# One level of Strassen's algorithm for the first products of seven batches, with other products between its steps

## Chip, cores, metric

One core of a Trainium2 chip. The metric is the device time of one execution in microseconds. "Faster" or "slower" means by over 2%.

## The reference

Cross attention between tokens and a small state, then a two-layer network on all rows, in f32.

```python
B, H, S, Ns, D = 8, 8, 512, 32, 64                 # x: (8,8,512,64), state: (8,8,32,64)
a = softmax(x @ state.T / sqrt(D)); xread = a @ state
a2 = softmax(state @ x.T / sqrt(D)); sread = a2 @ x
rows = concatenate([xread, sread], axis=2)         # then (B,H,S,D) -> (B*S, 512)
h = rows @ w_in                                    # 512 -> 2048
g = h * erf(softplus(h))
out = g @ w_out                                    # 2048 -> 512
```

The kernel never forms xread. For each batch it multiplies state and w_in once (a "mixed" product, `m`), so that the **first product** of a batch is h = a x m with a contraction of 256, and the **second product** is g x w_out. Both are large; Softplus, Erf and the multiplication lie between them.

## The kernel before

TensorE (PE) works through units: one unit is (batch, half of the tokens, half of the hidden features), four a batch. In a unit the first product is made tile by tile (`hidden`), then Softplus, Erf and the multiplication follow on ACT and DVE, and meanwhile PE does the second product of the unit before (`project7`, already by Strassen: 7 products for 8). Instructions are written in order of importance; the building step moves some of them ahead where it expects an engine to wait, and fixes one order for each engine.

```python
def mixed_part(b, g, j, parts):                    # L253, L255: two PSUM banks of the pool "at" (2)
    ps = [ps_at.tile([P, gw], F32, name="at")[:, 0:n] for _ in range(2)]
    for i in range(NI):
        for e in range(2):
            ...
            nc.tensor.matmul(out=ps[e][q, :], lhsT=stT[b][r, q], rhs=w_in[r, fs, i, :], ...)
    return nc.scalar.copy(mg[:, 0], ps[0]), nc.vector.tensor_copy(mg[:, 1], ps[1])

def hidden(b, fts, t0, n, copies=(nc.vector.tensor_copy,) * 4):
    ...
    for i in range(4):
        hp = ps_h.tile([P, S], F32, name="h")      # pool of 2 banks
        for j in range(m):
            ...                                    # two matmuls of 256 columns
        banks.append((nc.scalar.activation(out=s[:, i, :], in_=hp, func=ACTF.Softplus),
                      copies[i](hs[:, i, :], hp), on_pe))
    def finish():
        return (nc.scalar.activation(out=s, in_=s, func=ACTF.Erf),
                nc.vector.tensor_tensor(s, s, hs, op=ALU.mult))

def project7(gT, hs, g, first, last, acc):
    A11, A12, A22, S1, S2, S3, S4 = combine_g(gT, hs)     # four DVE sums of 128x512
    for lhs, rhs, bank, c in ((A11, B11, 2, 0), (A12, B21, 0, 0), (A22, T[4], 1, 0),
                              (S2, T[2], 0, 1), (S3, T[3], 2, 1), (S1, T[1], 1, 1),
                              (S4, B22, 3, 0)):
        for i in range(GF):
            nc.tensor.matmul(...)                  # 256 columns

# the loop over units
gT_ = first()
gT_[2]()                                           # Erf, multiplication
pending()                                          # second product of the unit before (and, every
...                                                # other time, store7: 5 DVE additions, 1 ACT copy)
if b + 1 < B:
    mixed(b + 1, g)                                # one mixed product after each unit
    if g == 1:
        attention(b + 1)[0]()
```

## Time and profile before

809.8 us is the median of four runs (808.86 to 810.66). A group is: line, engine, operation, output<-inputs, shape, count | busy us, mean ns of one | idle time ahead of it and what ended it.

```profile
L270 PE MATMUL h<-aT,m 128*128 128x256 f32 (+1 forms) x960 | 241.7, 399 | 4.5 <-DVE hs L273 2.5
...
L253 PE MATMUL at<-w_in,stT 64*32 64x512 f32 (+1 forms) x528 | 37.2, 588 | 0.7 <-ACT m L255 0.5
```

The first products are 30% of the span. The mixed products take 37.2 us of PE.

### The profile page before, as it was taken

Reading aid. Unit: us, or ns where it says so; the run is one execution under the profiler, and the core shown is the slowest. Engines: PE = TensorE matmul, PEld = TensorE weight load, DVE = VectorE, ACT = ScalarE, POOL = GpSimd, SP = SyncE. Lnnn points to the kernel's source line nnn. Section 1 sums busy time; section 2 is a strip of 40 time slices with the busy share of each in tenths; the row PEclk is TensorE's granted clock in tenths of the full one; section 3 lists DMA queues with packets and bytes.
Section 4 is the critical chain, followed back from the end, with each engine's and each line's share of the span. In section 5 each row is a group of like instructions: output and inputs, shape, how many; then the busy total and the mean of one; then the engine's idle time right before and its main releaser. Section 6 shows DMA issues by size and latency. Waiting matters only on the chain.

```text
span 810.8 us, 10642 instructions
## 1 busy us (share of the span) xinstructions
PE 792.5 (98%) x4532; PEld 611.7 (75%) x4532; DVE 427.9 (53%) x624; ACT 369.3 (46%) x466; POOL 0.7 (0%) x6
## 2 busy tenths in 40 slices
PE   8988999999999999999999999999999999999997
PEld 6533445687888788878887888878887888888886
DVE  3888854546454744555453844455455745443431
ACT  5858544655343733354334533373334533333220
POOL 0000000000000000000000000000000000000000
PEclk9999999999999999999999999999999999999999
DMA  6665521203000020003000200000000000000000
GB/s 211 208 229 186 126 49 56 53 1 79 0 27 1 8 71 1 27 1 78 1 27 1 47 32 1 27 1 27 1 27 0 27 1 26 1 27 1 26 1 26
DMA packets 47414, 35.27 MB, mean 44 GB/s; under 512 B 36872, under 2 KB 36872, under 8 KB 47368
## 3 DMA queue, kind: packets, MB, share of 16 engines
q1 hardware_dynamic: 45256, 34.09, 13.6%
q10 hardware_dynamic: 2112, 0.52, 0.3%
q8 instruction: 35, 0.57, 0.3%
q14 instruction: 11, 0.09, 0.0%
HBM read 25.69 MB, written 8.91 MB: 43 GB/s over the span
## 4 chain that ended last, share of the span: by engine, by line
PE 88%; ACT 3%; DVE 1%; DMA 1%; issue 1%; SPq 0%
PE o L335 45%; PE h L270 29%; PE o L283 5%; PE at L253 4%; PE at L156 1%; DMA raw<-in_moe_w_in_dram 1%; PE at L214 1%; PE at L226 1%; PE at L179 1%; PE at L197 1%; ACT L272 1%; ACT s L276 0%; ACT s L272 0%; ACT L276 0%; ACT xT L158 0%
## 5 line engine op out<-in xcount | busy, mean ns | idle before, releaser
L270 PE MATMUL h<-aT,m 128*128 128x256 f32 (+1 forms) x960 | 241.7, 399 | 4.5 <-DVE hs L273 2.5
L270 PEld LDWEIGHTS h<-aT,m 128*128 128x128 f32 x960 | 178.0, 190 | 67.5 <-issue 32.8
L273 DVE COPY hs<-h 128x512 f32<-128x512 f32 x134 | 91.9, 690 | 185.2 <-ACT s L272 185.1
L272 ACT ACTIVATE s<-h 128x512 f32<-128x512 f32 x136 | 80.2, 597 | 160.5 <-PE h L270 159.9
L277 DVE TENSOR_TENSOR s<-s,hs 128x2048 f32<-128x2048 f32 x34 | 77.9, 2293 | 75.8 <-ACT s L276 75.7
L335 PE MATMUL o<-w_out,s 128*128 128x256 f32 x480 | 114.9, 380 | 1.6 <-DVE s L277 1.6
L335 PE MATMUL o<-raw,hs 128*128 128x256 f32 x480 | 115.6, 380 | 0.0
L335 PE MATMUL o<-w_out,hs 128*128 128x256 f32 x480 | 113.4, 379 | 0.0
L335 PEld LDWEIGHTS o<-w_out,s 128*128 128x128 f32 x480 | 90.2, 190 | 14.3 <-DVE s L277 2.5
L335 PEld LDWEIGHTS o<-w_out,hs 128*128 128x128 f32 x480 | 91.1, 190 | 12.3
L335 PEld LDWEIGHTS o<-raw,hs 128*128 128x128 f32 x480 | 90.3, 190 | 12.4
L255 ACT COPY m<-at 128x512 f32<-128x512 f32 (+1 forms) x33 | 18.9, 573 | 154.1 <-PE at L253 154.0
L276 ACT ACTIVATE s<-s 128x2048 f32<-128x2048 f32 x34 | 64.9, 1910 | 0.4
L283 PE MATMUL o<-w_out,s 128*128 128x512 f32 x128 | 59.2, 600 | 0.9 <-DVE s L277 0.9
L335 PE MATMUL o<-raw,s 128*128 128x256 f32 x240 | 56.7, 379 | 0.0
L272 ACT ACT_TABLE_LOAD x40 | 51.3, 1283 | 0.7
L335 PEld LDWEIGHTS o<-raw,s 128*128 128x128 f32 x240 | 45.2, 190 | 5.9
L255 DVE COPY m<-at 128x512 f32<-128x512 f32 (+1 forms) x33 | 22.3, 675 | 50.6 <-PE at L253 50.5
L283 PEld LDWEIGHTS o<-w_out,s 128*128 128x128 f32 x128 | 23.1, 190 | 31.6 <-issue 30.4
L276 ACT ACT_TABLE_LOAD x34 | 43.6, 1283 | 0.6
L253 PE MATMUL at<-w_in,stT 64*32 64x512 f32 (+1 forms) x528 | 37.2, 588 | 0.7 <-ACT m L255 0.5
L346 ACT COPY m<-o 128x256 f32<-128x256 f32 x15 | 5.6, 373 | 57.3 <-PE o L335 57.3
(72 smaller groups left out, 583.4 us busy)
## 6 DMA issues: line engine op xcount, KB each, us to landing
raw<-in_moe_w_in_dram SPq DMA_DIRECT2D x8, 1024.0 KB, 5.4
raw<-in_moe_w_out_dram SPq DMA_DIRECT2D x8, 1024.0 KB, 5.8
out_dram<-ot SPq DMA_DIRECT2D x32, 256.0 KB, 2.3
x<-in_x_dram SPq DMA_DIRECT2D x60, 128.0 KB, 2.8
x<-in_x_dram ACTq DMA_DIRECT2D x4, 128.0 KB, 4.5
out_dram<-ot SPq DMA_DIRECT2D x8, 64.0 KB, 1.7
st<-in_state_dram SPq DMA_DIRECT2D x8, 56.0 KB, 4.3
st<-in_state_dram SPq DMA_DIRECT2D x2, 32.0 KB
```

The source lines that it names most:

```text
L156: nc.tensor.transpose(out=xp[:, P * c:P * c + P], in_=xt[:, c, 2 * i:2 * i + 2, :], identity=ident)
L179: on_pe = nc.tensor.transpose(out=s1[:, NI * c:NI * c + NI, :], in_=sc[:, e, P * c:P * c + P], identity=ident)
L197: nc.tensor.transpose(out=ps[:, P * c:P * c + P], in_=a[:, e, NI * c:NI * c + NI, :], identity=ident)
L253: nc.tensor.matmul(out=ps[e][q, :], lhsT=stT[b][r, q], rhs=w_in[r, fs, i, :], start=True, stop=True)
L255: return nc.scalar.copy(mg[:, 0], ps[0]), nc.vector.tensor_copy(mg[:, 1], ps[1])
L270: on_pe = nc.tensor.matmul(out=hp[:, n * j:n * j + n], lhsT=lhsT, rhs=rhs, start=(k == 0), stop=(k == len(ops) - 1))
L272: banks.append((nc.scalar.activation(out=s[:, i, :], in_=hp, func=ACTF.Softplus), copies[i](hs[:, i, :], hp), on_pe))
L273: copies[i](hs[:, i, :], hp), on_pe))
L276: return (nc.scalar.activation(out=s, in_=s, func=ACTF.Erf), nc.vector.tensor_tensor(s, s, hs, op=ALU.mult))
L277: nc.vector.tensor_tensor(s, s, hs, op=ALU.mult))
L283: nc.tensor.matmul(out=acc[r], lhsT=gT[:, i, P * r:P * r + P], rhs=w_out[:, GF * g + i, :], start=(g == 0 and i == 0), stop=(g == NG - 1 a ...
L335: nc.tensor.matmul(out=acc[bank][:, E2 * c:E2 * c + E2], lhsT=lhs[:, i, :], rhs=rhs[:, g, i, :], start=(first and i == 0 and c == 0), stop ...
```

## The change

Intent: the first product of batches 1 to 7 by Strassen's algorithm too: 7 products of half size instead of 8. The operand sums of m and a are made once per batch (`combine_m`, `combine_a`); three sums of results are made by accumulating in PSUM; the steps of the waiting second product, now a generator, are put between the steps of the seven. To have memory for the sums, the mixed products of the next batch move: no longer one after each unit but two after each of the last two. Not shown below: the layout of g, the order of the four units of a batch (`begins`) and the tile of `a2T` change with it. The diff is cut; `...` marks the places.

```diff
-    mix = ctx.enter_context(tc.tile_pool(name="mix", bufs=6))
+    mix = ctx.enter_context(tc.tile_pool(name="mix", bufs=4))
...
+    def combine_m(b, g):
+        (X11, X12), (X21, X22) = (...)             # cut
+        tt(S1, X21, X22, op=ALU.add)
+        tt(S2, S1, X11, op=ALU.subtract)
+        tt(X21, X11, X21, op=ALU.subtract)
+        tt(S4, X12, S2, op=ALU.subtract)
+    def combine_a(b):                              # the same for a: T1, T2, T3, T4, of 128x256
...
+    def hidden7(b, g, h, between):
+        product(1, p)
+        nc.scalar.copy(m1, p)
+        product(6, q)
+        add(u2, m1, q)
+        between()
+        product(2, p, False)
+        nc.scalar.copy(c11, p)
+        product(7, q, False)
+        add(u3, m1, q)
+        softplus(0)
+        between()
+        p, q = (ps_h.tile([P, S], F32, name="h") for _ in range(2))
+        product(5, p)
+        add(c22, u3, p)
+        product(4, q)
+        add(c21, u3, q)
+        between()
+        product(3, p, False)
+        add(c12, u2, p)
+        for k in (3, 2, 1):
+            softplus(k)
...
             for i in range(GF):
+                if i % 2 == 0 and (bank, c) != (2, 0):
+                    yield
+                if i == 2 and lhs is A12:
+                    tt(S1, A21, A22, op=ALU.add)   # and S2, S3, S4
...
-            gT_ = first()
-            gT_[2]()
-            pending()
+            steps = pending()
+            gT_ = first(lambda: next(steps))
+            done(steps)
...
-                mixed(b + 1, g)
                 if g == 1:
                     attention(b + 1)[0]()
+                if g >= 2:
+                    mixed(b + 1, 2 * (g - 2 ^ begins(b + 1)))
+                    mixed(b + 1, 2 * (g - 2 ^ begins(b + 1)) + 1)
+                    combine_m(b + 1, g - 2 ^ begins(b + 1))
+                if g == 3:
+                    combine_a(b + 1)
```

More of the change, by code (lines that the diff above doesn't have):

```diff
@@ L209, in rest @@
                                      scale=scale, accum_out=z2[:, e:e + 1])
-            a2T = att.tile([P, 2, NC, P], F32, name="a2T")
+            a2T = att.tile([P, 2, NC, P], F32, name="sc")
             for e in range(2):
@@ L255, in mixed_part @@
         return nc.scalar.copy(mg[:, 0], ps[0]), nc.vector.tensor_copy(mg[:, 1], ps[1])
+    def combine_m(b, g):
+        (X11, X12), (X21, X22) = ([m_t[b, 2 * g + j][:, e] for e in range(2)] for j in range(2))
+        sx = mix.tile([P, 3, gw], F32, name="sx", bufs=2)
+        S1, S2, S4 = (sx[:, k] for k in range(3))
+        tt = nc.vector.tensor_tensor
+        tt(S1, X21, X22, op=ALU.add)
+        tt(S2, S1, X11, op=ALU.subtract)
+        tt(X21, X11, X21, op=ALU.subtract)
+        tt(S4, X12, S2, op=ALU.subtract)
+        X[b, g] = X11, X12, S4, X22, S1, S2, X21
@@ new lines, in combine_a @@
+    def combine_a(b):
+        Y = aT[b].rearrange("p e (h r t) -> p e r h t", h=2, r=2)
+        (Y11, Y12), (Y21, Y22) = ([Y[:, e, r] for r in range(2)] for e in range(2))
+        sy = keep.tile([P, 3, 2, P], F32, name="sy", bufs=1)
+        T1, T2, T4 = (sy[:, k] for k in range(3))
+        tt = nc.vector.tensor_tensor
+        tt(T1, Y12, Y11, op=ALU.subtract)
+        tt(T2, Y22, T1, op=ALU.subtract)
+        tt(Y12, Y22, Y12, op=ALU.subtract)
+        tt(T4, Y21, T2, op=ALU.subtract)
+        Ys[b] = Y11, Y21, Y22, T4, T1, T2, Y12
@@ new lines, with product, softplus @@
+    X, Ys = {}, {}
+    def hidden7(b, g, h, between):
+        hs = act.tile([P, 4, S], F32, name="hs")
+        s = act.tile([P, 4, S], F32, name="s")
+        c11, c12, c21, c22 = (hs[:, k] for k in range(4))
+        m1, u2, u3 = s[:, 3], c12, c21
+        def product(n, bank, first=True):
+            x, y = X[b, g][n - 1], Ys[b][n - 1][:, h]
+            for i in range(GF):
+                q = slice(P * i, P * i + P)
+                nc.tensor.matmul(out=bank[:, q], lhsT=x[:, q], rhs=y, start=(first and i == 0),
+                                 stop=(i == GF - 1), skip_group_check=not first)
+        def softplus(k):
+            nc.scalar.activation(out=s[:, k], in_=hs[:, k], func=ACTF.Softplus)
+        add = lambda o, x, y: nc.vector.tensor_tensor(o, x, y, op=ALU.add)
+        p, q = (ps_h.tile([P, S], F32, name="h") for _ in range(2))
[10 more added lines that the diff above has]
+        between()
+        p, q = (ps_h.tile([P, S], F32, name="h") for _ in range(2))
+        product(5, p)
[7 more added lines that the diff above has]
+            softplus(k)
+        return s, hs
@@ L271, in hidden, with finish @@
                                              start=(k == 0), stop=(k == len(ops) - 1))
-            banks.append((nc.scalar.activation(out=s[:, i, :], in_=hp, func=ACTF.Softplus),
-                          copies[i](hs[:, i, :], hp), on_pe))
-        def finish():
-            return (nc.scalar.activation(out=s, in_=s, func=ACTF.Erf),
-                    nc.vector.tensor_tensor(s, s, hs, op=ALU.mult))
-        return s, hs, finish, banks
+            part = lambda t: t[:, i, :]
+            if m == 2:
+                part = lambda t: t.rearrange("p (h r) (i2 i1 t) -> p h i2 i1 r t", r=2, i2=2,
+                                             i1=2)[:, i // 2, i % 2]
+                hp = hp.rearrange("p (i1 r t) -> p i1 r t", i1=2, r=2)
+            banks.append((nc.scalar.activation(out=part(s), in_=hp, func=ACTF.Softplus),
+                          copies[i](part(hs), hp), on_pe))
+        return s, hs, banks
+    def finish(s, hs):
+        return (nc.scalar.activation(out=s, in_=s, func=ACTF.Erf),
+                nc.vector.tensor_tensor(s, s, hs, op=ALU.mult))
     def project(gT, g, acc, rs=range(NC), ts=range(GF)):
@@ L312, in combine_w, with project7 @@
         return last
-    def combine_g(gT, hs):
-        gv = gT.rearrange("p (h i2) (i1 r t) -> p h (i2 i1) r t", h=2, i1=2, r=2)
-        S4 = hs.rearrange("p (k i2) (i1 t) -> p k (i2 i1) t", i2=1, i1=GF)
-        A11, A12, A21, A22 = (gv[:, h, :, r, :] for r in range(2) for h in range(2))
-        S1, S2, S3, S4 = (S4[:, k] for k in range(4))
-        tt = nc.vector.tensor_tensor
-        tt(S1, A21, A22, op=ALU.add)
-        tt(S2, S1, A11, op=ALU.subtract)
-        tt(S3, A11, A21, op=ALU.subtract)
-        tt(S4, A12, S2, op=ALU.subtract)
-        return A11, A12, A22, S1, S2, S3, S4
-    def project7(gT, hs, g, first, last, acc):
-        A11, A12, A22, S1, S2, S3, S4 = combine_g(gT, hs)
+    def project7(gT, hs, g, first, last, acc):
+        blocks = lambda t: [t[:, k].rearrange("p (i t) -> p i t", i=GF) for k in range(4)]
+        A11, A21, A12, A22 = blocks(gT)
+        S1, S2, S3, S4 = blocks(hs)
+        tt = nc.vector.tensor_tensor
         for lhs, rhs, bank, c in ((A11, B11, 2, 0), (A12, B21, 0, 0), (A22, T[4], 1, 0),
@@ L334, in project7 @@
             for i in range(GF):
+                if i % 2 == 0 and (bank, c) != (2, 0):
+                    yield
+                if i == 2 and lhs is A12:
+                    tt(S1, A21, A22, op=ALU.add)
+                    tt(S2, S1, A11, op=ALU.subtract)
+                    tt(S3, A11, A21, op=ALU.subtract)
+                    tt(S4, A12, S2, op=ALU.subtract)
                 nc.tensor.matmul(out=acc[bank][:, E2 * c:E2 * c + E2], lhsT=lhs[:, i, :],
@@ L376, in tiles, with begins @@
         return [ps_o.tile([P, d_model], F32, name="o%d" % r) for r in range(n)]
+    def begins(b):
+        return 1 - b % 2
     def fast(b, parts, put):
@@ L385, in project_, with first, done @@
                     box.extend(tiles(4))
-                project7(*gT[:2], g, k == 0, k == 1, box)
+                yield from project7(*gT, g, k == 0, k == 1, box)
                 if k == 1:
                     store7(box, put(h))
+            def first(g, h, between):
+                if b < B:
+                    gT = hidden7(b, g, h, between)
+                else:
+                    gT = hidden(b, range(2 * GF * g, 2 * GF * g + 2 * GF), 2 * P * h, 2 * P)[:2]
+                finish(*gT)
+                return gT
             for k in range(2):
-                g = k ^ (h & 1)
-                yield lambda g=g, h=h: hidden(b, range(2 * GF * g, 2 * GF * g + 2 * GF),
-                                              2 * P * h, 2 * P), \
+                g = k ^ h ^ begins(b)
+                yield lambda between, g=g, h=h: first(g, h, between), \
                     lambda gT, k=k, g=g, h=h, box=box: project_(gT, k, g, h, box)
+    def done(steps):
+        for _ in steps:
+            pass
     def begin(on_pe, on_act, on_dve):
@@ L414 @@
     behind(at[0], weights_out, 0)
-    gT, hs, finish, banks = hidden(0, range(GF), 0, S,
-                                   [nc.scalar.copy] * 2 + [nc.vector.tensor_copy] * 2)
+    gT, hs, banks = hidden(0, range(GF), 0, S,
+                           [nc.scalar.copy] * 2 + [nc.vector.tensor_copy] * 2)
     behind(banks[1][:1], weights_out, 1)
     behind(banks[3][2:], warm, 24)
-    at = finish()
+    at = finish(gT, hs)
     acc = tiles(NC)
@@ L425 @@
                 made = behind(at, weights_in, 2 + j)
-            project(gT, 0, acc, range(2))
+            done(project(gT, 0, acc, range(2)))
             at, = mixed(0, 1)
@@ L429 @@
             made = behind(at, weights_out, 3)
-            project(gT, 0, acc, range(2, 3))
+            done(project(gT, 0, acc, range(2, 3)))
         else:
@@ L434 @@
                 behind(banks[1][:2], weights_in, 5)
-                project(gT_, 0, acc, range(3, 4), range(GF - 1))
+                done(project(gT_, 0, acc, range(3, 4), range(GF - 1)))
             else:
@@ L440 @@
             if g == 2:
-                project(gT_, 0, acc, range(3, 4), range(GF - 1, GF))
+                done(project(gT_, 0, acc, range(3, 4), range(GF - 1, GF)))
             for j in range(2):
@@ L447 @@
             states(1)
-        gT_, (gT, hs, finish, banks) = gT, hidden(0, range(GF * g, GF * g + GF), 0, S)
-        at = finish()
+        gT_, (gT, hs, banks) = gT, hidden(0, range(GF * g, GF * g + GF), 0, S)
+        at = finish(gT, hs)
         if g == NG - 1:
@@ L452 @@
         if g > 1:
-            project(gT_, g - 1, acc)
+            done(project(gT_, g - 1, acc))
     last = combine_w()
@@ L456 @@
         mixed(1, g)
+    for g in range(2):
+        combine_m(1, g ^ begins(1))
     attention(1)[0]()
+    combine_a(1)
     def pending():
-        project(gT, NG - 1, acc)
+        yield from project(gT, NG - 1, acc)
         store(acc, lambda r, ot: put_x(0, r // 2)(r % 2, ot))
@@ L479, in pending @@
             def pending(gT=gT_, second=second):
-                second(gT)
+                return second(gT)
             if b + 1 < B:
-                mixed(b + 1, g)
                 if g == 1:
                     attention(b + 1)[0]()
-    pending()
+                if g >= 2:
[4 more added lines that the diff above has]
+                    combine_a(b + 1)
+    done(pending())
 _INS = ['x', 'state', 'moe_w_in', 'moe_w_out']
```

## The prediction

> **What bounds the kernel now.** I read the busy table and the chain that ended last on the page first.
>
> ```profile
> PE 792.5 (98%) x4532; PEld 611.7 (75%) x4532; DVE 427.9 (53%) x624; ACT 369.3 (46%) x466; POOL 0.7 (0%) x6
> ...
> PE 88%; ACT 3%; DVE 1%; DMA 1%; issue 1%; SPq 0%
> ```
>
> TensorE is busy 98% of the span, and 88% of the last chain is its own work. Next, the busy time of each engine by stretch: the first stage with the weights, the hand-over to batch 1, one whole batch in the middle, and batch 7 after its first unit.
>
> ```profile
> 0.00:121.00 121.00, 111.09 (x545) 56.44 (x553) 87.20 (x99) 76.19 (x89) 0.70 (x6) 0.99 0.54 168
> 121.00:160.00 39.00, 36.73 (x273) 22.13 (x258) 19.28 (x37) 20.95 (x34) 0.00 (x0) 1.00 0.22 60
> ...
> 289.20:378.30 89.10, 88.86 (x546) 72.20 (x538) 46.35 (x72) 40.18 (x52) 0.00 (x0) 1.00 0.09 27
> ...
> 665.70:742.00 76.30, 76.30 (x361) 67.14 (x354) 35.85 (x47) 30.07 (x32) 0.00 (x0) 1.00 0.04 14
> ```
>
> The columns are length, then PE, PEld, DVE, ACT and POOL busy with counts, clock, DMA share, GB/s. In a middle batch PE idles 0.24 us of 89.1, so what is cut from its work there is gained. The idle time lies in the first 121 us (10 us), the hand-over (2.3 us) and the tail, where this change cuts nothing. Busy time alone is not enough, because matmuls overlap; I need the pitch, start to start. The timeline of PE gives it from runs that nothing interrupts:
>
> ```profile
> 13.54 7.31 PE L135 MATMUL o<-ident 128*128 128x128 f32 x64
> ...
> 301.50 1.89 PE L335 MATMUL o<-raw,hs 128*128 128x256 f32 x8
> ```
>
> With the durations by form, 383 and 380 ns for 256 columns, 275 (median) for the 128 columns of L135: pitch of 256 columns = (1.89 - 0.38)/7 = 0.216 us; pitch of 128 columns = (7.31 - 0.275)/63 = 0.1117 us. L135 is the warm-up product, with a weight load of its own for each matmul (132 loads for 132 matmuls), the very form that the change will use: 128 rows, 128 weights, 128 moving columns, f32. So halving the columns costs 3.5% over half. Each f32 matmul of the program is two such instructions (L335: 30 calls of 28 products' pieces = 840, and the groups hold 3 x 480 + 240 = 1680).
>
> **What the Trainium skill says.** "TensorE: Matmul & The Clock Gate", section "Back-to-back issue gap", gives N/2.4 + 2.5 ns for one pass. The trace fits two passes for each f32 instruction: 512/2.4 + 2.5 = 215.8 for 256 columns, and 256/2.4 + 5 = 111.7 for 128. The same page, section "LDWEIGHTS (loading the stationary operand)", gives columns/1.2: 107 ns for 128 columns. So at 128 moving columns the load is as long as the product, and only just hides; in the trace the load of L135 lasts 190 ns or more and still keeps the 0.112 pitch, so loads overlap too. "VectorE: DVE Perf Modes", section "Why PSUM operands drop a tier", holds fp32 with a PSUM operand to the base rate; here the copy hs<-h takes 690 ns and the two-operand addition ot<-m,o 684, so an addition out of the accumulator costs no more than the copy it replaces. "ScalarE: Activation LUTs", section "What ACT_TABLE_LOAD costs", has 1283 ns; the trace has 1283, and the change makes no more switches, since all four Softplus of a unit still stand before its one Erf.
>
> **The change part by part.** A unit is (batch, half of the tokens, half of the hidden features); batches 1 to 7 have 28.
>
> Matmuls. Before: 8 feature tiles x 2 contraction pieces = 16 matmuls of 256 columns, 32 instructions x 0.2159 = 6.91 us. After: 7 products x 4 = 28 matmuls of 128 columns, 56 instructions x 0.1117 = 6.25 us. Saved 0.65 us a unit, x 28 = **18.3 us**: not an eighth (0.86), because of the fixed part of the pitch. Three of the sums (P2 onto P1's bank, P7 onto P6's, P3 onto P5's) are made by letting a later product accumulate on the bank of an earlier one, which adds no TensorE work. That alone gives 810.6 - 18.3 = 792.3.
>
> Sums in the unit. Before: 4 copies out of PSUM on DVE, 0.69 each, and 4 Softplus on ACT. After: 5 DVE additions (3.45 us against 2.76) and 2 ACT copies (0.59 each) besides the 4 Softplus, which now read SBUF. Sums of the operands: per batch 8 additions of 128x512 (0.69) and 4 of 128x256 (0.42), 7.2 us. So per batch DVE goes from 46.4 to 46.4 + 4 x 0.69 + 7.2 = 56.3 us, ACT from 40.2 to 40.2 + 8 x 0.59 = 44.9, beside 88.9 - 2.6 = 86.3 of PE. Neither is a bound in sum.
>
> Hand-overs. The order within a unit is P1, P6, filler of 8 instructions (1.73 us), P2 onto P1's bank, P7 onto P6's, filler of 4 (0.86), P5, P4 in fresh banks, filler of 4, P3 onto P5's. A product takes 8 x 0.112 = 0.89. P2 waits for the ACT copy of P1: has 0.89 + 1.73 = 2.6 us, needs some 0.2 + 0.59. P7 waits for u2: has 1.73 + 0.89 = 2.6, needs 0.2 + 0.69. P5, P4 and P3 have 0.86 + 0.89 = 1.75 each against 0.8 to 0.9. So in a plain unit each fits, with 0.9 us in hand for one other DVE instruction in front.
>
> The way to the second product. After P3: addition 0.69, last Softplus 0.60, table 1.28, Erf 1.91, multiplication 2.29, with semaphores some 7.2 us, up to 8.9 if the four operand sums of the waiting second product stand ahead of that addition. PE has meanwhile 20 of the 28 matmuls of the waiting second product, 40 x 0.216 = 8.6, then P1 and P6 of the next unit, 1.8: 10.4 us. It fits with 1.5 us or more in hand.
>
> Moved work. The mixed products (L253, some 1.05 us each with the switch) of the next batch move from one after every unit to two after each of the last two. In the middle that is the same sum. At the hand-over it is a loss. Before, in the stretch from 149 to 156.4 us, PE had h and two mixed products of batch 2 to do while the first Softplus-Erf chain of batch 1 ran, and still waited 1.6 us for it. After, those 2.1 us of filler are gone, the products of unit 2 stop sooner (P2 needs a copy on ACT, which is at Erf), and combine_a (T1 and T2, 0.84 us) stands before P6. I estimate +1.7 us net of what is saved there.
>
> Collisions. Between batches the DVE does combine_m (4 x 0.69 = 2.75) just when u2 of the next unit is wanted. With the second mixed copy landing about 1.9 us after P1 starts, u2 is done about 5.35 and P7 wants it at 5.4. In the attention unit DVE has 9.7 us more to do. I put 0.3 to 0.4 us a batch on these, x 6 = 2 us.
>
> Sum: 810.6 - 18.3 + 1.7 + 2 = **796.0 us**, 1.8% faster.
>
> **Rivals.**
> 1. The engines that must answer between the products set the pace. Five hand-overs a unit instead of bank releases; every 1 us lost a unit is 28 us, so at 0.65 us a unit the gain is eaten and the time is 810; at 1 us it is 820. For it: DVE order is fixed when the program is built, and in the attention unit two or three other instructions of 0.69 can stand in front of u2 or u3. Against: fillers are there just for this, and in the kernel before, the same kind of release (a bank from DVE) is met in the middle of a unit without a gap in the pitch, since L335 pieces fill in.
> 2. At 128 columns the weight load no longer hides at the joints of products, where an instruction waits on a semaphore. The first matmul after an interruption has 0.32 instead of 0.216 to its next (as after a mixed product). If every one of 7 joints cost such 0.1 us, 28 x 7 x 0.1 = 20 us, and the time stays at 812. Against: joints of h and o, with waits that are met, show the plain 0.216 in the trace; whether this holds at 0.112 no line of before shows.
> 3. No loss at all: the mixed products and the fillers keep PE full at the hand-over too. 792.3, faster by 2.25%.
>
> **Range and chances.** The sure part is the arithmetic of the pitch, 18.3 us. The line of 2% is at 794.4, so it needs losses under 2.1 us in all; the hand-over takes most of this by my estimate, so rival 3 or near it has about 0.27. Rivals 1 and 2 in full have some 0.04 for slower by 2%; in part they stretch the upper end, as a loss of 0.3 us a unit gives 801. Range 792.3 to 802; faster 0.27, within 2% 0.69, slower 0.04.
>
> **What would show each step.** Right: the matmuls of the new products are 1568 of 128x128 with a pitch of 0.112 us, so 8 in 1.06 us with the tail; a middle batch takes 86.4 to 87 us and PE idles under 0.7 of it; DVE is at about 56 us in it. Idle PE time ahead of the new products with a DVE or ACT releaser is some 2 us in all; the stretch to the second product of batch 1 has 3 to 4 us of idle PE. Wrong: a pitch of 0.12 or more or a gap at each joint (rival 2); several us of PE idle before P7, P4 or P3, released by DVE (rival 1); PE waiting on the multiplication before the second product in every unit, which would mean the 10.4 us were not there because the built order puts fillers elsewhere.

## The result, and the profile after

797.73 us median of four runs (797.63 to 798.49); ratio to before 0.9853, 95% interval 0.9836 to 0.987. Faster by 1.5%, so within 2%. The page:

```profile
PE 781.4 (98%) x5204; PEld 625.8 (79%) x5204; DVE 485.2 (61%) x736; ACT 395.9 (50%) x516; POOL 0.7 (0%) x6
...
PE 89%; ACT 2%; DVE 2%; DMA 1%; issue 1%; SPq 0%; DVEq 0%; ACTq 0%
...
L253 PE MATMUL at<-w_in,stT 64*32 64x512 f32 (+1 forms) x528 | 43.9, 588 | 0.8 <-ACT m L255 0.5
```

PE is still the bound. But the mixed products, which are the same 528 instructions of the same mean length, are busy 43.9 us instead of 37.2. That is the first sign of where part of the gain went. Busy time by stretch, hand-over to batch 1 and one middle batch (columns as in the prediction):

```profile
113.81:152.50 38.69, 37.60 (x313) 23.87 (x312) 25.09 (x47) 22.76 (x38) 0.00 (x0) 1.00 0.30 79
...
304.91:392.61 87.70, 87.59 (x636) 74.50 (x635) 54.42 (x89) 43.75 (x59) 0.00 (x0) 1.00 0.09 25
```

A middle batch takes 87.70 us, not the 86.4 to 87 of the forecast, though PE seems to idle for 0.11 us of it. In the hand-over it idles for 1.09 us, not the 3 to 4 of the forecast.

**A ledger by units.** The weight and start stages take a different time in every execution: the first L226 instruction (a product of batch 0's attention) comes at 113.86 us in the trace before and between 110.10 and 113.03 in the others. In most of the later ones the granted clock up to there was lower (0.97 in e1, at 113.03; 1.00 in the changed kernel, at 110.10). From that instruction to the end the same kernel gives the same time: 685.84 us for the changed kernel in two profiles on different occasions. So I compare from there, and mark the end of each second product (the start of the 56th, 112th, ... instruction of its line on PE). The length of an interval in a middle batch, from the marks:

```
us                      plain   attention   third   fourth   batch    first L226 to end
before                  20.21   28.32       20.21   20.32    89.06    696.99
changed                 18.34   26.53       21.79   21.05    87.71    685.84
batch 7: before 18.99, changed 18.34 for each unit (no next batch to prepare)
```

One mixed product with its switch costs 20.21 - 18.99 = 1.22 us. So the changed kernel should have 18.34; 28.32 - 0.65 - 1.22 = 26.45; 18.34 + 2 x 1.22 = 20.78; and 20.89 (with 0.11 for the transposed state, as before). The third interval has 1.01 us too much, the fourth 0.16, the attention interval 0.08: 1.25 a batch. The timeline where the third interval begins, at 365.96 (start, length, engine, line, what; idle time ahead in brackets):

```profile
362.23 2.29 DVE L356 TENSOR_TENSOR s<-s,hs 128x2048 f32<-128x2048 f32 x1 [3.92 <-ACT s L355]
...
364.44 0.68 DVE L421 TENSOR_TENSOR ot<-m,o 128x512 f32<-128x512 f32 x1
364.44 1.89 PE L411 MATMUL o<-w_out,hs 128*128 128x256 f32 x8
365.04 0.68 DVE L407 TENSOR_TENSOR hs<-s 128x512 f32<-128x512 f32 x1
365.64 0.41 DVE L421 TENSOR_TENSOR u<-ot,o 128x256 f32<-128x256 f32 x1
365.97 0.68 DVE L408 TENSOR_TENSOR hs<-hs,s 128x512 f32<-128x512 f32 x1
366.26 1.09 PE L253 MATMUL at<-w_in,stT 64*32 64x512 f32 x16
366.57 0.68 DVE L421 TENSOR_TENSOR ot<-u,o 128x512 f32<-128x512 f32 x1
...
367.44 0.59 ACT L255 COPY m<-at 128x512 f32<-128x512 f32 x1 [4.15 <-PE at L253]
367.50 0.68 DVE L409 TENSOR_TENSOR hs<-s 128x512 f32<-128x512 f32 x1
368.10 0.41 DVE L421 TENSOR_TENSOR ot<-ot,o 128x256 f32<-128x256 f32 x1
368.15 2.11 PE L253 MATMUL at<-w_in,stT 64*32 64x512 f32 x16
368.43 0.68 DVE L255 COPY m<-at 128x512 f32<-128x512 f32 x1
```

The first mixed product (366.26) fills both banks of the pool. ACT copies one at once (367.44). DVE gets to the other only at 368.43, because the multiplication, store7 (L421) and the operand sums of the next second product (L407 to L410) stand in front. The second mixed product has begun at 368.15, with one matmul into the free bank; the rest waits for the DVE copy, which ends at 369.11. The group of 16 then lasts 2.11 us instead of 1.09. Because the one early matmul counts as busy, the wait hides in the busy time. The instructions of L253, asked for their waits (weight loads included), name it:

```profile
  DVE m L255: 6.3, 7
```

Seven times, 6.3 us: six in the loop and one at the hand-over.

### The profile page after: what moved, and what is told of

Its sections match the earlier page's. It is cut to its first block, busy times and chain, and to the rows that moved or that the text cites. A ratio compares the mean times of both kernels' runs of the same rounds, so it can differ in the third digit from the quotient of the medians.

```text
span 795.9 us, 12199 instructions
## 1 busy us (share of the span) xinstructions
PE 781.4 (98%) x5204; PEld 625.8 (79%) x5204; DVE 485.2 (61%) x736; ACT 395.9 (50%) x516; POOL 0.7 (0%) x6
## 4 chain that ended last, share of the span: by engine, by line
PE 89%; ACT 2%; DVE 2%; DMA 1%; issue 1%; SPq 0%; DVEq 0%; ACTq 0%
PE o L411 46%; PE h L299 22%; PE h L343 6%; PE at L253 5%; PE o L361 4%; PE at L156 2%; PE at L166 1%; PE at L214 1%; DMA raw<-in_moe_w_in_dram 1%; PE at L226 1%; PE at L179 1%; PE at L197 1%; ACT s L355 0%; ACT sc L216 0%; ACT L355 0%
## 5 line engine op out<-in xcount | busy, mean ns | idle before, releaser
L299 PEld LDWEIGHTS h<-aT,m 128*128 128x128 f32 x672 | 84.7, 191 | 27.5 <-issue 20.1
L303 ACT ACTIVATE s<-hs 128x512 f32<-128x512 f32 x112 | 70.6, 630 | 54.7 <-DVE hs L304 54.4
L299 PE MATMUL h<-aT,m 128*128 128x128 f32 x672 | 92.3, 280 | 0.0
L411 PEld LDWEIGHTS o<-w_out,s 128*128 128x128 f32 x480 | 85.2, 191 | 8.8 <-DVE s L356 0.5
L304 DVE TENSOR_TENSOR hs<-hs,h 128x512 f32<-128x512 f32 x84 | 57.6, 686 | 44.6 <-PE h L299 44.1
L299 PE MATMUL h<-sy,sx 128*128 128x128 f32 x448 | 62.0, 275 | 0.1
L299 PEld LDWEIGHTS h<-sy,sx 128*128 128x128 f32 x448 | 58.1, 192 | 1.7 <-DVE hs L304 0.4
L304 DVE TENSOR_TENSOR hs<-s,h 128x512 f32<-128x512 f32 x56 | 38.3, 683 | 32.7 <-PE h L299 32.7
L361 PEld LDWEIGHTS o<-w_out,s 128*128 128x128 f32 x128 | 23.1, 190 | 31.6 <-issue 29.6
L312 ACT COPY hs<-h 128x512 f32<-128x512 f32 x28 | 16.3, 581 | 58.2 <-PE h L299 58.2
L253 PE MATMUL at<-w_in,stT 64*32 64x512 f32 (+1 forms) x528 | 43.9, 588 | 0.8 <-ACT m L255 0.5
```

The lines of the kernel that those rows point to most:

```text
L299: nc.tensor.matmul(out=bank[:, q], lhsT=x[:, q], rhs=y, start=(first and i == 0), stop=(i == GF - 1), skip_group_check=not first)
L303: nc.scalar.activation(out=s[:, k], in_=hs[:, k], func=ACTF.Softplus)
L304: add = lambda o, x, y: nc.vector.tensor_tensor(o, x, y, op=ALU.add)
L312: nc.scalar.copy(c11, p)
L361: nc.tensor.matmul(out=acc[r], lhsT=gT[:, i, P * r:P * r + P], rhs=w_out[:, GF * g + i, :], start=(g == 0 and i == 0), stop=(g == NG - 1 a ...
L411: nc.tensor.matmul(out=acc[bank][:, E2 * c:E2 * c + E2], lhsT=lhs[:, i, :], rhs=rhs[:, g, i, :], start=(first and i == 0 and c == 0), stop ...
```

## The experiments

Each is the changed kernel with one edit, except where noted; all gave the right result. The ledger for all of them (middle batch, as above):

```
us                      plain   attention   third   fourth   batch    first L226 to end
a0 changed, again       18.34   26.53       21.79   21.05    87.71    685.84
e1 first early          18.34   28.16       20.86   19.75    87.11    682.19
e2 ACT copies           18.34   26.53       21.19   21.05    87.11    682.26
e3 old products         18.99   27.15       21.43   21.54    89.11    696.78
e4 no between           18.71   26.72       21.25   21.03    87.71    687.64
e5 slow answer          18.34   26.49       22.19   21.20    88.22    688.90
e7 own banks            18.34   26.49       22.14   21.03    88.00    688.69
e8 sums after copy      18.34   26.53       20.85   21.03    86.75    680.16
e9 both                 18.34   26.53       20.85   21.03    86.75    680.14
```

**a0: the changed kernel again**, on the chip of e1 to e3.

> The changed kernel itself, on the chip of the three runs sent with it, so that they can be compared with it. 797.7 us within 1 us. All theories agree.

799.35 us median (797.81 to 799.57), 0.9869 of before. 1.6 us more than the first time, so the 1 us was missed. The execution that was profiled is the fastest, 797.81, with the same start stage and the same ledger; the other three had a slightly lower clock (0.996 and 0.997 against 0.999) and no profile. Between the profiles of all runs the start stage alone differs by up to 3.8 us, so differences of 1 or 2 us in time say little here, and the ledger is used.

**e1: the first of each pair of mixed products earlier.**

```diff
             gT_ = first(lambda: next(steps))
+            if b + 1 < B and g >= 2:
+                mixed(b + 1, 2 * (g - 2 ^ begins(b + 1)))
             done(steps)
...
-                    mixed(b + 1, 2 * (g - 2 ^ begins(b + 1)))
```

> The first of each pair of mixed products of the next batch is asked for before the rest of the second product instead of after it, so that some 9 us of other products lie between the two. Theory A (of the 1.25 us that each middle batch lost against my sum, 1.0 us is the second mixed product of the third unit waiting for a PSUM bank, since the DVE copy of the first one stands behind store7 and the operand sums): 6 batches x 1.0 us come back, less 6 x 2 x 0.1 for two more switches, so 792 to 793.5 us, and the unit of marker 7 falls from 21.79 to about 20.8. Theory B (the lost time is the answers of DVE and ACT between the seven products, and the wait at the mixed product only shows where PE happens to stand): the wait moves elsewhere, 797 us or more.

794.88 us, 0.9815 of before (0.9795 to 0.9835: on which side of 2% is unclear), between what the two theories said. In the ledger 3.65 us less than the changed kernel. The third interval fell from 21.79 to 20.86 as theory A said, and the wait on the DVE copy is down to one. But the mixed product that moved into the attention interval costs 28.16 - 26.53 = 1.63 us there instead of 1.22, so 0.60 a batch came back, not 0.9.

**e2: both copies of the pair's first mixed product on ACT**, in the third interval.

```diff
+                    mixed(..., second=nc.scalar.copy if g == 2 else nc.vector.tensor_copy)
```

> In the third unit both banks of the first mixed product are copied by ACT, the second no longer by DVE; nothing else moves. In the trace of the changed kernel the DVE copy begins at 368.43 and ends 369.11, ACT's ends at 368.03, so two ACT copies would end at some 368.6. Theory A: 0.5 us a batch come back, 3 us in all, some 794.7 us. Theory B: no change, 797.7.

795.65 us, 0.9829 of before; 3.58 us less in the ledger, all of it in the third interval (21.79 to 21.19). Theory A's 0.5 a batch was 0.6. So PE waits for that copy, and an earlier copy shortens the time by as much.

**e3: the old first products in the changed kernel.**

```diff
-                if b < B:
-                    gT = hidden7(b, g, h, between)
-                else:
-                    gT = hidden(...)[:2]
+                gT = hidden(...)[:2]
-                    combine_m(...)                 # and combine_a, and those of batch 1
```

> The changed kernel with the old first products (16 matmuls of 256 columns a unit, four copies) and without the operand sums; the moved mixed products, the unit order and everything else stay. Theory A: the matmuls are worth 18.3 us, and the wait of the pair stays since it has to do with the order of mixed and store alone: 797.7 + 18.3 = 816 us, so slower than the kernel before by some 6. Theory B: without the five answers a unit there is no loss: about 809 to 810, as the kernel before.

810.4 us, 1.0012 of before (0.9987 to 1.0036): here theory A failed, in one of its parts. I had put the wait down to the place of the pair alone, and it is not there with the old products in five of the six batches: third interval 21.43 = 20.21 + 1.22, exactly. The plain interval is 18.99, so the matmuls are worth their 0.65. The DVE in the same place:

```profile
362.97 2.29 DVE L356 TENSOR_TENSOR s<-s,hs 128x2048 f32<-128x2048 f32 x1 [2.91 <-ACT s L355]
...
370.19 0.41 DVE L421 TENSOR_TENSOR ot<-ot,o 128x256 f32<-128x256 f32 x1
...
371.20 1.09 PE L253 MATMUL at<-w_in,stT 64*32 64x512 f32 x16
371.31 0.42 DVE L421 TENSOR_TENSOR ot<-ot,o 128x256 f32<-128x256 f32 x1 [0.71 <-PE o L411]
...
372.43 0.69 DVE L255 COPY m<-at 128x512 f32<-128x512 f32 x1 [0.69 <-PE at L253]
```

With the old products the multiplication ends 5.9 us ahead of the mixed product (365.26 to 371.20), DVE has done all its sums, stands idle and copies at once. With the new ones it ends 1.7 us ahead (364.52 to 366.26): from the end of the first product to the pair PE has 8.7 us of other work, not 12.7. With the fillers 16 instructions of the second product come ahead of that end, with the old products 10 (1.3 us), and most of the rest is attention's L214 and L226, which also come ahead of it now. So 4 us less remain to cover Erf, multiplication, operand sums and store7. In batch 1 of e3, the exception, the multiplication ends only 1.95 us ahead of the pair, and there the wait appears with the old products too: 22.04 us. The theory mended: not the pair alone, nor the new products as such, but the pair behind a DVE that is late.

**e8: only the order of DVE changed.** The operand sums of the next second product are held behind the DVE copy of the pair's first mixed product. They are in no hurry: in the trace of the changed kernel the last of them ends at 369.72, and PE first reads one at 381.05.

```diff
                 if i == 2 and lhs is A12:
-                    tt(S1, A21, A22, op=ALU.add)   # and S2, S3, S4
+                    with ExitStack() as order:
+                        for m in copied:           # the DVE copy of the pair's first product
+                            order.enter_context(tc.issue_after(m.ins))
+                        tt(S1, A21, A22, op=ALU.add)   # and S2, S3, S4
+                    copied.clear()
...
-                    mixed(b + 1, 2 * (g - 2 ^ begins(b + 1)))
+                    copied[:] = [mixed(b + 1, 2 * (g - 2 ^ begins(b + 1)))[0][1]]
```

> The changed kernel with the order of DVE alone altered: in the units with a pair of mixed products the four operand sums of the next second product (which nobody wants for some 6 us) are held until the DVE copy of the pair's first product has been issued. PE's order is untouched. After the third run my theory A stands corrected: with the old products the wait of the pair is not there, so it is not the pair's place alone, but that Erf and the multiplication now end 1.7 us ahead of the unit's end (5.9 with the old products), so store7 and the operand sums, 5.2 us of DVE, hang over into the mixed products. Then taking 2 us of these away ends the wait: 1.0 us a batch, 6 us in all, from the first L226 to the end 679.8 us instead of 685.84. If the wait has another cause, 685.8 stays.

792.79 us (792.02 to 794.66), ratio 0.9788, interval 0.9765 to 0.9811. In the ledger 680.16, where 679.8 was expected. In the traces PE and ACT have the same order of instructions as before the edit; only DVE's differs. The place in question:

```profile
366.97 1.09 PE L253 MATMUL at<-w_in,stT 64*32 64x512 f32 x16
...
368.19 0.69 DVE L255 COPY m<-at 128x512 f32<-128x512 f32 x1 [0.21 <-PE at L253]
368.80 0.68 DVE L412 TENSOR_TENSOR hs<-s 128x512 f32<-128x512 f32 x1
368.85 1.17 PE L253 MATMUL at<-w_in,stT 64*32 64x512 f32 x16
```

DVE now waits for PE, not PE for DVE; the second mixed product takes 1.17 us instead of 2.11, and L253's waits on this copy fall to one:

```profile
  DVE m L255: 1.0, 1
```

This settles the cause of 5.7 us of the loss. What is left of it, some 1.4 us over the whole, was not followed up.

**e4: no other products between the steps.**

```diff
-            gT_ = first(lambda: next(steps))
+            gT_ = first(lambda: None)
```

> The seven products of a unit are asked for in one piece, without other products between their steps; the building order may still put some in where it sees a gap. My theory: each answer needs 0.8 to 0.9 us and a product gives 0.89, so 0.1 us is lost at up to three joints, 0.2 to 0.4 a unit (18.34 becomes 18.6 or so), 6 to 11 us in 28 units; but multiplication and store end 3 us sooner, so the 1.0 us of the pair's wait is gone, 6 us. Net 0 to 5 us slower than the changed kernel. The rival of the prediction (answers set the pace, only the fillers hide them): 0.7 us or more a unit, 20 us slower, back to the kernel before.

800.92 us, 0.9887 of before, 1.8 us over the changed kernel in the ledger: within the forecast. A plain unit is 18.71, so the written fillers are worth 0.37 us there (in the trace the build has put no instruction of the second product between the seven by itself). And in the middle batch the third interval is 21.25 = 18.71 + 2.44 + 0.10: the pair's wait is all but gone, since the multiplication now ends 3.1 us ahead of the pair. In batch 1, where it ends 2.2 us ahead, the interval is 22.03; in one other batch it is 21.51. The fillers give 0.37 in a plain unit, 0.19 in the attention interval and nothing in the fourth, and take 0.9 back in the third.

**e5: later answers.**

```diff
+        add(c22, m1, m1)                           # needless
         add(u2, m1, q)
...
+        add(c22, m1, m1)                           # needless
         add(u3, m1, q)
```

> One needless DVE addition of 0.69 us directly ahead of u2 and one ahead of u3 in each of the 28 units: each answer is 0.69 us later. By the prediction's slack (2.6 and 1.75 us against 0.9) a plain unit stays at 18.34; in the units with attention or mixed products, where DVE is behind already, up to 1.4 us a batch may show, so 0 to 8 us slower in all. If the answers set the pace: 1.38 x 28 = 39 us slower, or 19 if one of the two shows.

802.19 us, 0.9908 of before, 3.1 us over the changed kernel in the ledger. A plain unit stays at 18.34 to the hundredth. But the edit did less than was meant. Both needless additions need only m1, so DVE does them while it waits for PE anyway. The answers u2 and u3 (`hs<-s,h`) in a unit of batch 7, in the changed kernel:

```profile
692.32 0.69 DVE L304 TENSOR_TENSOR hs<-s,h 128x512 f32<-128x512 f32 x1 [0.94 <-PE h L299]
695.76 0.69 DVE L304 TENSOR_TENSOR hs<-s,h 128x512 f32<-128x512 f32 x1 [2.75 <-PE h L299]
```

and in e5, where `hs<-s` are the needless ones:

```profile
696.65 0.69 DVE L304 TENSOR_TENSOR hs<-s 128x512 f32<-128x512 f32 x1 [0.59 <-ACT s L307]
697.26 0.68 DVE L304 TENSOR_TENSOR hs<-s,h 128x512 f32<-128x512 f32 x1
697.86 0.69 DVE L304 TENSOR_TENSOR hs<-s 128x512 f32<-128x512 f32 x1
700.44 0.69 DVE L304 TENSOR_TENSOR hs<-s,h 128x512 f32<-128x512 f32 x1 [1.90 <-PE h L299]
```

From the mark ahead (690.05 and 694.72) u2 comes 0.3 us later and u3 no later. So answers that are 0.69 us late were not tested in a plain unit. What the run adds is 1.4 us of DVE work a unit, and its cost falls in the third and fourth intervals, where DVE is late: the multiplication ends 0.9 us ahead of the pair there instead of 1.7.

**e7: a bank for each product**, sums by DVE.

```diff
-        product(2, p, False)
-        nc.scalar.copy(c11, p)
-        product(7, q, False)
-        add(u3, m1, q)
+        p = ps_h.tile([P, S], F32, name="h")
+        product(2, p)
+        add(c11, m1, p)
+        q = ps_h.tile([P, S], F32, name="h")
+        product(7, q)
+        add(u3, u2, q)
...                                                # and product 3 likewise, one addition more
```

> Undoes the accumulation: every one of the seven products gets a bank of its own, and the sums c11, u3, c12 are all made by DVE (two additions more a unit, 1.38 us, and one ACT copy less). Work of PE is the same. My theory: a plain unit stays at 18.34 or within 0.2 of it, since the fillers still cover the answers; the DVE's work at the end of the unit is later by up to 1.4 us, so the wait of the pair grows from 1.0 by 0.7 to 1.4 us a batch: 4 to 8 us slower than the changed kernel. If the accumulation were worth nothing: equal to the changed kernel.

802.08 us, 0.9905 of before, 2.9 us over the changed kernel in the ledger, less than the 4 to 8 that I wrote: the third interval grew by 0.35 only, and 1.19 came at the hand-over (43.61 us from the first L226 to the first second product of batch 1, against 42.42), which I had not named. A plain unit stays at 18.34. So the accumulation in PSUM saves nothing in a plain unit; it keeps work off a DVE that is late elsewhere.

**e9: e8, and at the hand-over combine_m of batch 1 after attention instead of before it.**

```diff
-    for g in range(2):
-        combine_m(1, g ^ begins(1))
     attention(1)[0]()
+    for g in range(2):
+        combine_m(1, g ^ begins(1))
     combine_a(1)
```

> The eighth kernel (operand sums held behind the DVE copy of the pair) and, besides, the sums of batch 1's weights (combine_m, 8 additions) asked for after attention of batch 1 instead of before it. In the trace of the changed kernel the last mixed product of the hand-over also waits 1.1 us for a DVE copy that stands behind those additions. If that wait is on the path to the first unit, interval 0 falls from 42.42 to some 41.4 and the whole from 680.16 to 679.1; if attention's own chain ends later for another reason, or products of batch 0 fill the wait anyway, interval 0 stays. By time 791 to 793 us, 2.1 to 2.3% under the kernel before.

793.0 us over five rounds, ratio 0.9793, interval 0.978 to 0.9806. The hand-over stays at 42.42 and the whole at 680.14, but this decides nothing: in the traces of e8 and e9 PE, ACT and DVE have the same instructions in the same order, so the building step undid the edit, and the seventh wait for a DVE copy (1.0 us) is still there. Whether it is on the path stays open. e9 is e8 run again. Both are faster than the kernel before by some 2.1%; as both intervals reach across 0.98, "faster" by the definition above is unclear. Against the changed kernel the ledger shows 5.7 us.

## Why the prediction was right, step by step

796.0 was said and 797.73 measured, in the range; "within 2%", said with 0.69, came. That it came so near is partly luck. From the first L226 on, the traces differ by 11.15 us; the sum said 14.6. Of its three terms one was exact and two were mis-sized, in opposite directions:

- **Matmuls, -18.3.** Right. A unit of batch 7 falls from 18.99 to 18.34, the 0.65 of the sum. The pitch of 0.112 holds across the joints of products. In the timeline of the changed kernel, P2 and P7 in a row; P7 needs the answer u2, which had come:

```profile
285.43 1.95 PE L299 MATMUL h<-aT,m 128*128 128x128 f32 x16
```

  (1.95 - 0.275)/15 = 0.1117. Rival 2, a gap at each joint, falls with it. The sum rests on the measured pitches alone.
- **Hand-overs within a unit fit.** Right: a plain unit is 56 x 0.1117 + 56 x 0.2157 = 18.33 us of pitches, and takes 18.34, so PE waits nowhere in it. In the trace u2 ends 1.7 us before P7 begins, and u3 and c22 (the sum that frees the bank for P3) 0.9 us before P4 and P3. Rival 1 falls, in its form of 0.65 us or more a unit. e4, without fillers, loses 0.37, so the fillers are needed.
- **The way to the second product, 10.4 us against 7 to 9.** Right as far as it went: in a plain unit it is 6.9 us from the end of P3 to the end of the multiplication, and apart from the hand-over PE does not wait for it. (The prediction's upper figure of 8.9 counts 1.7 us for four operand sums that it elsewhere puts at 2.75; in the trace they run long before that addition, so nothing hung on it.) What it left out is what queues behind the multiplication on DVE.
- **Collisions, +2 us (0.3 to 0.4 a batch).** This term failed in size, and in the place. It was 7.4: 6 x 1.01 in the third interval, some 0.9 in the fourth and 0.4 in the attention intervals. I looked for the collision at combine_m and u2; PE shows no such wait, as the built order has u2 ahead of three of the four sums of combine_m. It was at the DVE copy of the first of two mixed products back to back. Shown by e2 (copy elsewhere, 3.58 us back) and e8 (sums out of its way, 5.68 back). The causes of the 0.9 and the 0.4 were not sought.
- **Hand-over, +1.7 us.** Failed, in its sign. From the first L226 to the second mark the changed kernel is 4.62 us shorter; three units of 0.65 and two mixed products that moved out of this stretch are 4.40. So the hand-over cost -0.2. I had said that two mixed products were the filler for the first Softplus-Erf chain and would be missed. The wait ahead of the first second product, before and after:

```profile
156.40 1.13 PE L335 MATMUL o<-w_out,s 128*128 128x256 f32 x4 [1.59 <-DVE s L277]
```

```profile
148.86 0.82 PE L156 MATMUL at<-ident,x 128*128 128x128 f32 x6
...
152.52 3.72 PE L411 MATMUL o<-w_out,s 128*128 128x256 f32 x16 [0.23 <-DVE s L356]
```

  It shrank from 1.59 to 0.23; the building step put transposes of the next batch's x (L156) in the gap. In e3, without new products, the same stretch is 1.0 us shorter than the mixed products that left it account for. That the transposes are the reason is what the timeline suggests; no run took them away.

The two errors, -1.9 and +5.4, cancel in part. In time the difference is 12.1 us rather than 11.15, which is within what the start stage varies by. And the sum started from 810.6 where the median was 809.8. The forecast for a middle batch, 86.4 to 87 us, missed (87.70), mainly by the third interval; e8 has 86.75.

The forecast of DVE in a middle batch, 56 us, was 54.4: back-to-back additions of 128x512 start 0.60 us apart while each lasts 0.68, so their busy times overlap.

## What to carry to other kernels

When work moves to before the end of a stage, look at what is queued behind it on the engine that finishes the stage: here the gain on the bound engine was exact, and a third of it went back because an unhurried sum stood ahead of a copy that freed a PSUM bank. Holding that sum behind the copy gave 5.7 of 7.4 us back and touched nothing on the bound engine. Before a run is read, check in its trace that the edit reached the built program: e9's did not, and e5's delay was mostly swallowed by a wait. And compare units from mark to mark, not busy shares: one early matmul of a group hides the wait of the rest in the busy time.

## What the Trainium skill lacked or had wrong

- "TensorE: Matmul & The Clock Gate", section "Back-to-back issue gap", has no f32 figure: here an f32 product is two matmul instructions, each with a pitch of 0.216 us at 256 columns and 0.1117 at 128. At 128 a weight load of its own for each instruction still hides, in the warm-up product and across the joints of the seven.
- "ScalarE: Activation LUTs", section "What ACT_TABLE_LOAD costs", puts a drain of some 1380 ns to the 1283 of a table load. In the changed kernel's trace a Softplus ends at 358.97 us, a load starts at 358.99 and Erf at 360.29: 1.32 us in all, with no drain on either side.
- "VectorE: DVE Perf Modes", section "The DRAIN you can't avoid", first says that the next instruction does not start until the pipe is empty, then that one which isn't held starts earlier. Here the second holds, with a number that the section lacks: additions of 128x512 f32 in a row start 0.60 us apart and last 0.68 each.
- "Perfetto Trace Analysis", section "Identifying the Most-Contended Engine", warns that the busy time of matmuls is no good measure of how near a kernel is to its bound, because they are pipelined. It lacks the reason met here: a group of tiled matmuls that waits for its second PSUM bank after one early matmul shows as 2.11 us busy instead of 1.09, and seven such waits raised that line from 37.2 to 43.9 us.
